# A causal convolution in front of two gated layers: two products of tile 1 made on GpSimd

## The chip, the core and the metric

The kernel runs on one core of a Trainium2 chip. A core has TensorE (matrix products, PE in the rows), VectorE (DVE), ScalarE (ACT), GpSimd (POOL), SyncE (SP, which issues the transfers here) and 16 DMA engines. All share one on-chip memory of 128 partitions (SBUF); TensorE writes its sums to a second one (PSUM, 8 banks). The metric is device microseconds of one execution of the whole kernel, median of several runs; lower is better.

## What is computed

```python
w = softmax(weight_gen, axis=-1)             # (2, 4096, 8 heads, 7 taps)
x_pad = concat([zeros((B, 6, D)), x], axis=1)
out[b, s, h, :] = sum_k w[b, s, h, k] * x_pad[b, s + k, h, :]   # 24 channels a head, D = 192
x = out.reshape(8192, 192)
x = (silu(x @ w_gate) * (x @ w_val)) @ w_out          # 192 -> 1536 -> 192
h = x @ w_in                                          # 192 -> 2048
return (h * clip(h + 3, 0, 6) / 6) @ w_out2           # 2048 -> 192
```

Each position gets its own seven tap weights for each of eight heads; the sum of the seven products goes through two layers. The layers' matrix products are made with each operand split into a high and a low part, so one product of the reference is three on TensorE.

## The kernel before

**Tiles and blocks.** The 8192 positions are 16 tiles of 512 (128 partitions x 4 positions, 768 numbers a partition). A tile's layer 1 is 12 blocks of 128 hidden columns, its layer 2 is 8 blocks of two such groups. The blocks run tiles 0 and 1 in turns of four (blocks 0 to 3 are tile 0's, 4 to 7 tile 1's), then tiles 2 and 3, then layer 2 of one tile and layer 1 of a later one in turn. In a layer 1 block TensorE makes `pg` and `pv` (L661, 18 matrix products, two at a time on the two halves of the array), ScalarE the silu (`p`, L695), VectorE multiplies by `pv` (L698), ScalarE makes the high part `gh` (L674), VectorE the low part `gl` (L703), and two or three blocks later TensorE multiplies these by `wo` (L742).

**Turns.** The two halves of the array write both banks in turn. `Turn` (L589) hands over: an empty instruction in GpSimd's queue waits for both halves' last product of the first part, and the second part on TensorE waits for that instruction. Each block has one or more, in block order, and apart from a few memsets at the start GpSimd has nothing else to do.

**Weights.** They come as float64 and are made into a high and a low fp32 part in chunks: ScalarE takes the exponent (L243), VectorE shifts (L249) and joins the words (L252, L258), ScalarE writes the high part (L309 for `wi`, L327 for `wo`), VectorE the low part (L294). A block waits for its chunk.

**Convolution.** A tap is one VectorE product of 128x768 (L390), 24 channels a weight. From tile 2 on the seven products are added on VectorE. Tiles 0 and 1 are needed before there is other work, and TensorE adds part of theirs: `TERMS[t]` lists groups of taps; within a group VectorE adds (L457), and each group's sum is a *term*, which TensorE multiplies by a unit matrix into two PSUM banks (L467, eight matrix products of fp32, 16 in the trace). Tile 1 has three terms, of taps 6+5, 4+3 and 2+1+0: seven products and four sums on VectorE.

**Order.** Everything is issued in an order that a planner in the kernel makes when it is built: it keeps a clock for each engine (`V["A"]`, `V["D"]`, `clock`), fills each engine's queue between a block's steps with items of the convolution (`c`) or of the weights (`w`), and puts terms into TensorE's queue when its clock has come to their time (`late_pe`). Each engine then works through its queue in order. While tile 1 has no term begun, the planner also fills time in which it expects TensorE to wait with products of the unit matrix that nobody reads (`heat`, L502, called at L624).

Of the kernel before, what the change touches and what calls it, by code (L numbers as in the profile page):

```python
# [8 lines left out]
F32 = mybir.dt.float32  # L9
# [29 lines left out]
def conv_swiglu_relu6_kernel(  # L39
# [11 lines left out]
    nc = tc.nc  # L51
    P = 128
    B, S, D = x.shape
# [12 lines left out]
    MJ = 4  # L66
# [2 lines left out]
    GBUFS = 4  # L69


    TERMS = [[[6], [5], [4], [3, 2], [1, 0]], [[6, 5], [4, 3], [2, 1, 0]]]

    START = [(0, 4), (4, 8), (8, 12)]
    SPREAD = (0, 4)
# [30 lines left out]
    V = {"A": 2000.0, "D": 2800.0, "Q": 1000.0}  # L106
    late_act, late_exp, late_pe, urgent = [], [], [], []
# [61 lines left out]
    def v_cost(cols):  # L169
        return 1.042 * cols + 70  # L170
# [40 lines left out]
    pools, late = {}, {}  # L211
# [166 lines left out]
    def after_taps(t):  # L378

        if t + 2 < T:  # L380
            before = load_x(t + 2)
            if before:
                before()
        if t == groups[t // GT][-1]:
            load_wg(t // GT + 2)

    def taps(eng, t, k, o, a=0, b=None):

        b = b or sizes[t]
        eng.tensor_mul(  # L390
            o.rearrange("p j (h g) -> p j h g", h=H),
            xt_t[t][:, a + k:b + k, :].rearrange("p j (h g) -> p j h g", h=H),
            wg_t[t][:, a:b, :, k:k + 1].broadcast_to([P, b - a, H, G]),
        )
# [39 lines left out]
    def conv_pe_items(t):  # L434


        n = sizes[t]
        box, count, items = {}, [0], []
        c = v_cost(n * D)

        def step(k, tag):
            def go():
                if tag == "acc":
                    o = vp.tile([P, MJ, D], F32, tag="acc", name="acc", bufs=1)
                else:
                    count[0] += 1
                    src = vp if count[0] % 2 else pools["c"]
                    o = src.tile([P, MJ, D], F32, tag="tmp", name="tmp", bufs=2)
                box[tag] = o
                taps(nc.vector, t, k, o[:, :n, :])  # L450
                if k == TERMS[t][-1][-1]:
                    after_taps(t)
            return go

        def add():
            o = box["tmp"][:, :n, :]
            nc.vector.tensor_add(o, o, box["acc"][:, :n, :])  # L457

        def pe(first, last):
            o = box["tmp"]  # L460

            def go():
                if first:
                    pe_t[t] = [acc_bank(0), acc_bank(2)[:D2]]
                for dst, a, b in zip(pe_t[t], (0, P), (P, D)):
                    for s in range(n):
                        nc.tensor.matmul(  # L467
                            dst[:, s * P:(s + 1) * P], o[:, s, a:b], ident,
                            start=first and s == 0, stop=last and s == n - 1,
                        )  # L470
            late_pe.append((go, V["D"]))

        for q, term in enumerate(TERMS[t]):
            items.append((c, step(term[0], "tmp")))
            for k in term[1:]:
                items += [(c, step(k, "acc")), (c, add)]
            _, f = items.pop()

            def both(f=f, first=q == 0, last=q == len(TERMS[t]) - 1):
                f()  # L480
                pe(first, last)
            items.append((c, both))
        return items
# [15 lines left out]
    def acc_bank(q):  # L499
        return ap.tile([P, MN], F32, tag=f"a{q}", name=f"a{q}")  # L500
# [389 lines left out]
    def due(q):  # L890
        tag = queues[q][0][0]
        if tag == ("c", 1):
            left = sum(x[0] == tag for x in queues["c"])
            return SPREAD[0] + SPREAD[1] * (1 - left / len(conv_pe_items(1)))
        return dues.get(tag, 0)
# [204 lines left out]
    with tc.manual_schedule():  # L1100
# [3 lines left out]
            c=w1.enter_context(tc.tile_pool(name="c1", bufs=2)),  # L1104
            n=768, ahead=4,
# [17 lines left out]
        add(("c", 0), s0)  # L1123
        until(("c", 0))
        taps0 = [(("c", 0), c, f, None) for c, f in conv_pe_items(0)]
        s1 = [(("c", -1), x[0], x[1], x[2] if len(x) > 2 else None) for x in s1]
        s2 = [(("c", -2), x[0], x[1], x[2] if len(x) > 2 else None) for x in s2]
        first = taps0[:1] + s1[:2] + taps0[1:]
# [18 lines left out]
        nc.scalar.activation(warm, three, AF.Silu)  # L1147
        on("A", 1300)
        add(("c", 1), conv_pe_items(1))
        queues["c"] += s2[2:]  # L1150
        add(("c", 2), conv_items(2))
# [4 lines left out]
        for ph in phases:  # L1156
            kind, t0, _ = ph[0]
            if kind == 2 and t0 + 4 < T:
                t = t0 + 4
# [46 lines left out]
```

## Time and profile before

| | |
|---|---|
| median of 3 runs (lowest to highest) | 1251.93 us (1250.68 to 1252.17) |
| profiled execution, its own time | 1249.53 us |
| span in its trace | 1247.5 us |
| TensorE busy | 1231.6 us, 99% |
| VectorE busy | 922.1 us, 74% |
| ScalarE busy | 674.9 us, 54% |
| GpSimd busy | 3.6 us |

A row of a timeline gives the start, the duration, the engine, the line, the operation and the tile names; in brackets stands the idle time before it and what ended that. Busy spans of neighbours may overlap by some hundredths, since an instruction starts before the one ahead has left. In the trace one fp32 matrix product by the unit matrix counts twice.

### The profile page before, as it was taken

The numbers are of one execution on the slowest core, as the hardware profiler recorded it, in microseconds if no ns is written. First come the engines' busy times: TensorE is split into PE (matmuls) and PEld (weight loads), VectorE is DVE, ScalarE is ACT, GpSimd is POOL, SyncE is SP. The second block draws the span as 40 slices with busy tenths as digits, with TensorE's granted clock in tenths as the row PEclk, the third lists the DMA queues.
The fourth block names the chain that finished last, engine by engine and source line by source line (L and its number), as shares of the span: only waits on it lengthen the run. The fifth ranks groups of instructions, "written<-read, shape, count | busy, mean of one in ns | idle before, by whom it ended". The sixth has DMA issues, their size and how long they took to land.

```text
span 1247.5 us, 29356 instructions
## 1 busy us (share of the span) xinstructions
PE 1231.6 (99%) x12104; PEld 1183.7 (95%) x12104; DVE 922.1 (74%) x1475; ACT 674.9 (54%) x1175; POOL 3.6 (0%) x11
## 2 busy tenths in 40 slices
PE   8899999999999999999999999999999999999998
PEld 7687878999999999999999999999999999999998
DVE  8889987986876848687595866959478694645665
ACT  3455565654655547465464546546465554645555
POOL 1000000000000000000000000000000000000000
PEclk9999999999999999999999999999999999999999
DMA  8313230011010100101001010100000000000000
GB/s 236 117 45 106 86 107 9 14 42 53 18 46 18 54 10 10 45 18 53 10 10 45 19 53 19 38 17 19 37 19 14 12 8 16 17 14 9 14 15 14
DMA packets 26725, 46.96 MB, mean 38 GB/s; under 512 B 3046, under 2 KB 19428, under 8 KB 26592
## 3 DMA queue, kind: packets, MB, share of 16 engines
q1 hardware_dynamic: 26592, 45.09, 12.3%
q8 instruction: 95, 1.56, 0.5%
q14 instruction: 38, 0.31, 0.1%
HBM read 30.92 MB, written 6.29 MB: 30 GB/s over the span
## 4 chain that ended last, share of the span: by engine, by line
PE 91%; DVE 5%; ACT 2%; DMA 1%; SPq 1%; issue 1%; DVEq 0%; ACTq 0%; POOLq 0%
PE ph L661 23%; PE a L822 21%; PE a L742 16%; PE pv L661 15%; PE pg L661 14%; DVE p L698 1%; DVE gl L703 1%; DVE f L252 0%; DMA xt<-in_x_dram 0%; DVE f L258 0%; DVE tmp L390 0%; ACT gh L674 0%; DMA raw<-in_moe_w_in_dram 0%; SPq L305 0%; DVE wi L294 0%
## 5 line engine op out<-in xcount | busy, mean ns | idle before, releaser
L661 PE MATMUL pg<-s,wi 64*128 64x512 f32 x1728 | 454.1, 395 | 6.1 <-ACT wi L309 2.5
L661 PE MATMUL pv<-s,wi 64*128 64x512 f32 x1728 | 425.1, 395 | 2.2 <-DVE p L698 1.1
L674 ACT ACTIVATE gh<-p 128x512 fp32r<-128x512 f32 x448 | 278.9, 633 | 216.9 <-DVE p L698 164.6
L661 PEld LDWEIGHTS pg<-s,wi 64*128 64x128 f32 x1728 | 307.1, 184 | 21.1 <-ACT wi L309 2.8
L661 PE MATMUL ph<-s,wi 64*128 64x512 f32 x2304 | 318.7, 393 | 1.2 <-DVE p L785 1.1
L661 PEld LDWEIGHTS pv<-s,wi 64*128 64x128 f32 x1728 | 297.1, 184 | 14.9 <-DVE p L698 2.5
L822 PE MATMUL a<-wo,gh 64*128 64x384 f32 x2016 | 311.0, 353 | 0.0
L822 PE MATMUL a<-wo,gl 64*128 64x192 f32 x2016 | 300.6, 247 | 0.0
L822 PEld LDWEIGHTS a<-wo,gh 64*128 64x128 f32 x2016 | 295.9, 184 | 0.3
L822 PEld LDWEIGHTS a<-wo,gl 64*128 64x128 f32 x2016 | 290.8, 187 | 0.0
L661 PEld LDWEIGHTS ph<-s,wi 64*128 64x128 f32 x2304 | 268.7, 184 | 3.3 <-DVE p L785 1.6
L742 PE MATMUL a<-gh,wo 64*128 64x512 f32 x1152 | 253.3, 392 | 0.8 <-ACT wo L327 0.7
L781 ACT ACTIVATE p<-ph,three 128x512 f32<-128x512 f32 x256 | 161.7, 684 | 126.5 <-PE ph L661 125.9
L698 DVE TENSOR_TENSOR p<-p,pv 128x512 f32<-128x512 f32 x192 | 131.8, 687 | 122.7 <-ACT p L695 121.5
L742 PE MATMUL a<-gl,wo 64*128 64x512 f32 x768 | 208.0, 392 | 0.0
L703 DVE TENSOR_TENSOR gl<-p,gh 128x512 fp32r<-128x512 f32 x192 | 132.6, 691 | 94.3 <-ACT gh L674 94.3
L695 ACT ACTIVATE p<-pg 128x512 f32<-128x512 f32 x192 | 114.5, 596 | 160.8 <-PE pg L661 159.7
L785 DVE SCALAR_TENSOR_TENSOR p<-p,ph 128x512 f32<-128x512 f32 x256 | 163.6, 680 | 46.2 <-ACT p L781 45.8
L795 DVE TENSOR_TENSOR gl<-p,gh 128x512 fp32r<-128x512 f32 x256 | 165.7, 689 | 13.1
L742 PEld LDWEIGHTS a<-gh,wo 64*128 64x128 f32 x1152 | 161.8, 184 | 9.0 <-ACT wo L327 1.4
L742 PEld LDWEIGHTS a<-gl,wo 64*128 64x128 f32 x768 | 115.7, 184 | 4.1
L390 DVE TENSOR_TENSOR tmp<-xt,wg 128x768 f32<-128x768 f32 x92 | 87.0, 953 | 0.7
(66 smaller groups left out, 509.1 us busy)
## 6 DMA issues: line engine op xcount, KB each, us to landing
xt<-in_x_dram SPq DMA_DIRECT2D x14, 960.0 KB, 4.9
out_dram<-o SPq DMA_DIRECT2D x15, 384.0 KB, 2.3
s<-s SPq DMA_DIRECT2D x16, 256.0 KB, 2.9
s<-s SPq DMA_DIRECT2D x56, 64.0 KB, 2.0
raw<-in_moe_w_out_dram SPq DMA_DIRECT2D x8, 384.0 KB, 3.2
raw<-in_moe_w_out_dram SPq DMA_DIRECT2D x3, 768.0 KB, 7.0
raw<-in_moe_w_in_dram SPq DMA_DIRECT2D x16, 128.0 KB, 2.4
wg<-in_weight_gen_dram SPq DMA_DIRECT2D x7, 224.0 KB, 5.0
```

The costliest lines, as they stand in the source:

```text
L390: eng.tensor_mul(o.rearrange("p j (h g) -> p j h g", h=H), xt_t[t][:, a + k:b + k, :].rearrange("p j (h g) -> p j h g", h=H), wg_t[t][:, a ...
L661: return nc.tensor.matmul(ps[b][:, :N], w[rows, s, m, c], x[rows, l, :N], start=start, stop=stop)
L674: nc.scalar.activation(gh[:, :N], p[:, :N], AF.Copy)
L695: nc.scalar.activation(p[:, :N], pg[:, :N], AF.Silu)
L698: nc.vector.tensor_mul(p[:, :N], p[:, :N], pv[:, :N])
L703: nc.vector.tensor_sub(gl[:, :N], p[:, :N], gh[:, :N].bitcast(F32))
L742: return nc.tensor.matmul(y[:, :N], wo1[rows, i, col:col + P], x[rows, :N], start=start, stop=stop)
L781: nc.scalar.activation(q, ph[:, :N], AF.Relu, bias=three)
L785: nc.vector.scalar_tensor_tensor(out=q, in0=q, scalar=6.0, in1=ph[:, :N], op0=ALU.min, op1=ALU.mult)
L795: nc.vector.tensor_sub(gl[:, :N], q, gh[:, :N].bitcast(F32))
L822: return nc.tensor.matmul(z[s][:, :w], x[rows, s * P:(s + 1) * P], late["wo2"][rows, blk, :w], start=start, stop=stop,)
```

## The change

Taps 1 and 0 leave tile 1's last term. GpSimd makes their two products into two tiles of their own (`pt`), and each becomes a term of its own for TensorE, put into its queue behind tile 1's first term. VectorE loses two products and two sums of 128x768; TensorE gets five terms of tile 1 in place of three. All other code is the same; since the planner's clocks move, the order around it does too.

```diff
-    TERMS = [[[6], [5], [4], [3, 2], [1, 0]], [[6, 5], [4, 3], [2, 1, 0]]]
+    TERMS = [[[6], [5], [4], [3, 2], [1, 0]], [[6, 5], [4, 3], [2]]]
+    POOL_TAPS = [[], [1, 0]]
...
+        pooled = []
+
+        def pool_taps():
+            for k in POOL_TAPS[t]:
+                o = pools["c"].tile([P, MJ, D], F32, tag="pt", name="pt", bufs=2)
+                taps(nc.gpsimd, t, k, o[:, :n, :])
+                pooled.append((o, V["D"] + 2400 * (len(pooled) + 1)))
...
-            late_pe.append((go, V["D"]))
+            late_pe.append((go, at or V["D"]))
+            if first:
+                for x, when in pooled:
+                    pe(False, False, x, when)
+
+        if POOL_TAPS[t]:
+            items.append((0, pool_taps))
```

On GpSimd the two products stand behind the turn of block 0 and ahead of the turn of block 1. They wait for the softmax weights of tile 1 (VectorE, L371).

On VectorE, from tile 1's first tap to the product `p` of block 1 (`wi_84<-f_239` is the low part of block 1's weights, `f_251` the chunk of blocks 2 and 3), before:

```order
L390 TENSOR_TENSOR tmp<-xt_131,wg_103 128x768
L390 TENSOR_TENSOR acc<-xt_131,wg_103 128x768
L249 TENSOR_SCALAR f_251<-f_251 128x768
L698 TENSOR_TENSOR p<-p,pv 128x512
L457 TENSOR_TENSOR tmp<-tmp,acc 128x768
L703 TENSOR_TENSOR gl<-p,gh 128x512
L294 SCALAR_TENSOR_TENSOR wi_84<-f_239,wi_84 128x3x128
L390 TENSOR_TENSOR tmp<-xt_131,wg_103 128x768
L390 TENSOR_TENSOR acc<-xt_131,wg_103 128x768
L457 TENSOR_TENSOR tmp<-tmp,acc 128x768
L698 TENSOR_TENSOR p<-p,pv 128x512
```

and now:

```order
L391 TENSOR_TENSOR tmp<-xt_131,wg_103 128x768
L391 TENSOR_TENSOR acc<-xt_131,wg_103 128x768
L250 TENSOR_SCALAR f_251<-f_251 128x768
L712 TENSOR_TENSOR p<-p,pv 128x512
L295 SCALAR_TENSOR_TENSOR wi_84<-f_239,wi_84 128x3x128
L717 TENSOR_TENSOR gl<-p,gh 128x512
L466 TENSOR_TENSOR tmp<-tmp,acc 128x768
L391 TENSOR_TENSOR tmp<-xt_131,wg_103 128x768
L712 TENSOR_TENSOR p<-p,pv 128x512
```

The low part of block 1's weights has moved ahead of a sum and of `gl`; one tap and one sum have left this stretch.

On TensorE, between blocks 1 and 2 (the last product of block 1, then the first two of block 2; `a_344` and `a_345` are the two banks of tile 1's sum), before:

```order
L661 MATMUL pg<-s_254,wi_84 128x512
L467 MATMUL a_344<-ident,tmp 128x128 x4
L467 MATMUL a_345<-ident,tmp 64x128 x4
L661 MATMUL pg<-s_254,wi_84 128x512
L661 MATMUL pv<-s_254,wi_84 128x512
```

and now:

```order
L675 MATMUL pg<-s_254,wi_84 128x512
L521 MATMUL a_383<-ident 128x128 x19
L675 MATMUL pg<-s_254,wi_84 128x512
L675 MATMUL pv<-s_254,wi_84 128x512
L675 MATMUL pg<-s_254,wi_84 128x512
```

Tile 1's first term has left this place, and 19 products that nobody reads stand there. The `heat` between blocks 0 and 1 has 8 of them in place of 13.

On TensorE, between blocks 2 and 3 (`pv<-s_254` is the last of block 2), before:

```order
L661 MATMUL pv<-s_254,wi_84 128x512
L467 MATMUL a_344<-ident,tmp 128x128 x4
L467 MATMUL a_345<-ident,tmp 64x128 x4
L661 MATMUL pg<-s_254,wi_84 128x512
L661 MATMUL pv<-s_254,wi_84 128x512
```

and now:

```order
L675 MATMUL pv<-s_254,wi_84 128x512
L476 MATMUL a_428<-ident,tmp 128x128 x4
L476 MATMUL a_429<-ident,tmp 64x128 x4
L476 MATMUL a_428<-ident,pt 128x128 x4
L476 MATMUL a_429<-ident,pt 64x128 x4
L476 MATMUL a_428<-ident,pt 128x128 x4
L476 MATMUL a_429<-ident,pt 64x128 x4
L675 MATMUL pg<-s_254,wi_84 128x512
```

Three terms stand where one stood. Behind block 3, where the third term stood, the two others stand now. From tile 1's first block on TensorE's order is the same as before.

## Rows read from the trace of the kernel before

**Rows 1.** The profile page: busy time, share of the span and instructions.

```profile
PE 1231.6 (99%) x12104; PEld 1183.7 (95%) x12104; DVE 922.1 (74%) x1475; ACT 674.9 (54%) x1175; POOL 3.6 (0%) x11
```

**Rows 2.** Stretches: length, busy time and instructions by engine, granted clock, DMA share, GB/s.

```profile
32.40:34.90 2.50, 0.00 (x0) 0.00 (x0) 2.06 (x5) 1.54 (x2) 0.00 (x0) 0.93 0.00 0
34.90:38.60 3.70, 3.07 (x12) 1.67 (x12) 3.24 (x4) 1.76 (x2) 0.00 (x0) 0.59 0.71 210
53.00:60.00 7.00, 7.00 (x64) 5.62 (x62) 6.86 (x10) 3.37 (x5) 0.00 (x0) 1.00 0.42 115
300.00:600.00 300.00, 300.00 (x3010) 299.16 (x3008) 218.54 (x346) 162.76 (x283) 0.00 (x0) 1.00 0.10 28
```

**Rows 3.** TensorE's timeline, blocks 1 to 4: start, duration, operation, idle before.

```profile
23.43 3.17 PE L507 MATMUL a<-ident 128*128 128x128 f32 x26
28.01 0.50 PE L661 MATMUL pg<-s,wi 64*128 64x512 f32 x1 [0.74 <-DVE wi L294]
29.32 0.18 PEld L661 LDWEIGHTS pv<-s,wi 64*128 64x128 f32 x1 [0.55 <-POOLq L598]
30.21 2.18 PE L467 MATMUL a<-ident,tmp 128*128 128x128 f32 x16
34.91 0.79 PE L661 MATMUL pg<-s,wi 64*128 64x512 f32 x1 [2.52 <-ACT wi L309]
38.64 1.56 PE L742 MATMUL a<-gh,wo 64*128 64x512 f32 x3 [0.67 <-ACT wo L327]
41.07 2.18 PE L467 MATMUL a<-ident,tmp 128*128 128x128 f32 x16
43.17 0.49 PE L661 MATMUL pg<-s,wi 64*128 64x512 f32 x1
47.64 2.18 PE L467 MATMUL a<-ident,tmp 128*128 128x128 f32 x16 [0.71 <-DVE tmp L457]
49.75 0.49 PE L661 MATMUL pg<-s,wi 64*128 64x512 f32 x1
```

**Rows 4.** VectorE's timeline from tile 1's first tap to block 1's `p`.

```profile
23.12 0.96 DVE L390 TENSOR_TENSOR tmp<-xt,wg 128x768 f32<-128x768 f32 x1
25.33 0.68 DVE L698 TENSOR_TENSOR p<-p,pv 128x512 f32<-128x512 f32 x1
25.93 0.95 DVE L457 TENSOR_TENSOR tmp<-tmp,acc 128x768 f32<-128x768 f32 x1
26.80 0.68 DVE L703 TENSOR_TENSOR gl<-p,gh 128x512 fp32r<-128x512 f32 x1
27.40 0.55 DVE L294 SCALAR_TENSOR_TENSOR wi<-f,wi 128x384 fp32r<-128x384 f32 x1
30.95 0.69 DVE L698 TENSOR_TENSOR p<-p,pv 128x512 f32<-128x512 f32 x1 [0.27 <-ACT p L695]
```

**Rows 5.** GpSimd's operations by line and shape: busy us, mean ns.

```profile
L151 POOL MEMSET xt<- 1x1152 f32 x2 | 2.1, 1050 | 0.1
masks.py:199 POOL TENSOR_SCALAR_AFFINE_SELECT ident<-ident 128x128 f32<-128x128 f32 x1 | 0.3, 292 | 0.1
```

**Rows 6.** Timeline of the start: GpSimd's memsets, a VectorE operation beside them, one without.

```profile
1.28 3.06 POOL L151 MEMSET xt<- 1x1152 f32 x4
...
3.24 0.39 DVE L359 TENSOR_TENSOR wg<-wg,sm 128x224 f32<-128x224 f32 x1
...
6.82 0.39 DVE L359 TENSOR_TENSOR wg<-wg,sm 128x224 f32<-128x224 f32 x1
```

**Rows 7.** TensorE's waits from 110 to 320 us: total, times, longest.

```profile
PE pv L661 <- DVE p L698: 0.9, 1, 0.9
PE pg L661 <- ACT p L695: 0.7, 1, 0.7
PE pv L661 <- DVE s L574: 0.4, 1, 0.4
...
PE ph L661 <- DVE p L785: 1.1, 1, 1.1
```

More of the change, by code (lines that the diff above doesn't have):

```diff
@@ L457, in add, with pe @@
             nc.vector.tensor_add(o, o, box["acc"][:, :n, :])
-        def pe(first, last):
-            o = box["tmp"]
+        def pe(first, last, o=None, at=None):
+            o = o or box["tmp"]
             def go():
```

## The prediction

> **What bounds the kernel.** I read the busy line first: TensorE is busy 99% of the span, VectorE 74%, and GpSimd has 3.6 us of work [rows 1]. That is an average, so the stretches come next. From 53 us on TensorE has hardly a gap, and in the long middle none at all [rows 2]; what it waits for behind 110 us is 0.9 + 0.7 + 0.4 + 1.1 us in the four largest waits [rows 7]. So the end of the kernel is the time at which TensorE comes to tile 1's first block, plus work that the change leaves alone. Every microsecond by which block 4, at 49.75 [rows 3], comes later or earlier is one at the end. Before that block TensorE does wait, and its timeline names whom for [rows 3]: 0.74 us for the low part of block 1's weights, 2.52 us for the weights of block 2, 0.67 us for `wo`, 0.71 us for a sum of tile 1's taps. All four come from VectorE's queue, directly or through ScalarE.
>
> **What VectorE gives back.** Up to `p` of block 0 at 25.33 its queue stays as it is. Then the low part of block 1's weights came at 27.40, behind a sum and `gl` [rows 4]; now it is next, at 25.93 where the sum started. That is 27.40 - 25.93 = 1.47 us earlier. The shorter `heat` does not eat it: 26 products took 3.17 us, 0.122 each [rows 3], so 16 end at 23.43 + 1.95 = 25.4. Block 1 then ends at 30.21 - 1.47 = 28.74 instead of 30.21, its `p` and the chain of words behind it (which the change leaves in the same order) come 1.47 us earlier too, and so do block 2's start, from 34.91 to 33.44, and the wait for `wo` at 38.64. The 19 new `heat` products take 38 x 0.122 = 4.64 us from 28.74 and end at 33.38, just inside the wait. Block 2 ends at 41.07 - 1.47 = 39.60. The other tap and sum that leave VectorE stood late, ahead of the third term: the 0.71 us at 47.64 goes, since the second and third terms' sums are then ready before block 3 ends. Together -2.18 us.
>
> The clock: in the 2.5 us without a product the granted clock fell, and the stretch after it ran at a mean of 0.59 of 2.4 GHz, part of it at the lower level [rows 2]. `heat` now fills that gap. I cost this at nothing: block 2's first part, the one that ran slowly, ended in a wait for `wo` (0.67 us before 38.64), which VectorE's chain ends.
>
> **What TensorE gets.** A term takes 43.17 - 41.07 = 2.10 us [rows 3]. Before, the first of tile 1's three stood at 30.21 to 32.39, ahead of the wait that ended at 34.91: it cost nothing, the wait was its cover. That place now holds `heat`. All five terms now stand where TensorE has work behind them: three between blocks 2 and 3 where one stood, two behind block 3 where one stood. That is three more on the path, 3 x 2.10 = +6.30 us. Sum so far: 6.30 - 2.18 = +4.12 us at block 4.
>
> **What comes later.** VectorE has four operations of 0.95 us less, and TensorE is later. Behind 110 us the waits for `p` and its ScalarE part are 0.9 + 0.7 us [rows 7], at a place where convolution and weights crowd VectorE. They stand at a transposition that takes two of the four banks, so part remains whatever VectorE does. Bounds 0 and -1.6; I take -0.5, since the same crowd of weight steps stands there now, nearer to the first. The planner's new order could also add such a wait.
>
> **What the two products cost GpSimd.** No row shows a two-input product there. Below, VectorE's own tap: 0.96 us [rows 4]. The nearest GpSimd rows: a memset of 1152 numbers 1.05 us, which reads nothing, and a select of 128 in 0.292 us, which reads one input [rows 5]. Scaled by columns the select gives 768 / 128 x 0.292 = 1.75 us; twice that for two inputs, 3.5 us, is the upper bound. I take 1.75 us, the row on this engine that reads and writes. Both products together: 3.5 us from 23.1, until 26.6. What is queued behind them on GpSimd is block 1's turn: TensorE's second part of block 1 waits for it. It was taken at 29.32 after 0.55 us [rows 3], so it is asked for at 28.77 - 1.47 = 27.3. At 1.75 us each the products are through by then; at 3.5 us each they end at 30.1, and block 1 would be 2.8 us later.
>
> **What they cost VectorE.** Both engines then read SBUF at once, and no row shows that. The memsets ran beside a VectorE operation that took 0.39 us, as it did without them [rows 6], but a memset reads nothing. Bounds: no cost; or one engine at a time, both products whole ahead of block 1's weights, 2 x 1.75 = +3.5 us. I take sharing, each at half pace while both read: VectorE's work from 23.12 to the end of that low part is 26.48 - 23.12 = 3.36 us, of which 0.60 is `p`, which reads PSUM; the other 2.76 us doubles. The low part is 2.76 us later, GpSimd is done at about the same time (29.5 us), and block 1's turn is not later than its weights. I take this value rather than none because the work beside which the row shows no cost is of another kind, and rather than 3.5 because `p` leaves one gap. Everything behind, block 2 and its `wo`, hangs on that chain and takes the +2.76 us whole.
>
> Sum: 4.12 - 0.5 + 2.76 = **+6.4 us**. On the profiled execution's 1249.53 us that is 1255.9. The runs' median lies 2.4 us above that execution, so the forecast against it is 1251.93 + 6.4 = 1258.3 us.
>
> **A rule against the change.** In the trace before, VectorE and GpSimd never read SBUF together, and the memset beside `L359` cost nothing [rows 6]. The Trainium skill, "SBUF — State Buffer", section "Who interferes with whom", says that a VectorE instruction with two SBUF inputs contends with a GpSimd instruction that reads SBUF, though not with one that only writes it, and that the one which starts first holds the interface while the other fully blocks. The memset row agrees with its second half; no run here shows the first. By it the sum would be that of the first rival.
>
> **Rivals.** *One at a time.* An engine that has started holds the memory to the end of its instruction. The tap at 23.12 starts first, GpSimd's first product comes in behind it and its second behind VectorE's next: +3.5 us on the chain instead of 2.76, +7.1 us in all, 1259.0. If VectorE's back-to-back queue wins until `p` at 25.33, the second product waits until VectorE idles (about 30.1), block 1's turn with it until 31.9, and block 1 ends 0.55 + 0.89 us later at 33.3 instead of 28.74: +4.6, in all +8.2 us, 1260.1. For it: most of VectorE's queue there has two inputs in SBUF. Against it: nothing in the rows.
>
> *No interference.* +4.12 - 0.5 = +3.6 us, 1255.5. It needs products of under about 2.1 us each, or the turn is late.
>
> *Not slower: relief behind 110 us.* With no interference as well, VectorE's queue is so much shorter that all four late waits go, 0.9 + 0.7 + 0.4 + 1.1 = 3.1 us instead of 0.5 [rows 7]: 4.12 - 3.1 = +1.0 us, 1252.9. It decides if no wait for `p` is left at those places. Against it: the banks at the transpositions are taken as before.
>
> *Slow products.* 3.5 us each on GpSimd, and sharing: VectorE reads for 2.76 us up to the low part and for 2.34 more in `gl`, sum and tap, 5.1 in all, which take 10.2; with `p` that is until 33.9, when GpSimd has done 5.7 of 7.0 us. Its turn comes at 35.2, and block 1 ends 0.55 + 0.89 us later at 36.6 instead of 28.74: +7.9 us in place of 2.76, in all +11.5 us, 1263.4.
>
> **How the numbers follow.** Sharing 0.32, one at a time 0.25, no interference 0.20, relief 0.15, slow products 0.08. Sharing and one at a time lie within 2 us of each other, so the forecast is 1258.3. The range goes from 1253.5, between relief and no interference, to 1261.5, above one at a time: relief and slow products are left out, some 0.2. About 0.2% (2.5 us) is what a measurement of this kernel can tell from no change. Slower by more: sharing, one at a time, slow products and 0.12 of no interference, 0.77. Within it: 0.08 of no interference, whose 3.6 us may lose another 1.1 to a second late wait, and 0.09 of relief, 0.17. Faster by more than that: the rest of relief, if VectorE's queue also held TensorE back where no wait shows, 0.06.
>
> **What the profile after will show.** The two `pt` products on GpSimd near 23 us, with their duration. VectorE's rows beside them at 0.95 or longer. The wait for block 2's weights ending at 33.4 without interference, at 36 or more with it. Three terms in a row between blocks 2 and 3 and two behind block 3, 2.1 us each, without a wait of 0.71. Tile 1's first block at 49.75 + 4.1 to + 8.7. The rest at the same pace. I am wrong if TensorE finds idle time under the added terms, or if block 4 starts by 51 us.

## The result, and the profile after

The changed kernel takes 1259.68 us (median of 4 runs, 1259.03 to 1260.60) where the kernel before took 1251.31 us (4 runs, 1250.66 to 1252.17): a ratio of 1.0070 with a 95% interval of 1.0056 to 1.0084, slower by 8.4 us where 6.4 was forecast. The profiled execution's own time is 1259.27 us, its span 1257.5 us.

The busy line of the changed kernel's page answers to [rows 1].

```profile
PE 1242.3 (99%) x12164; PEld 1192.9 (95%) x12164; DVE 921.7 (73%) x1471; ACT 676.7 (54%) x1175; POOL 8.1 (1%) x13
```

VectorE has four instructions less and yet only 0.4 us less busy time; GpSimd has 4.5 us more. What the products did beside VectorE stands in the timelines of the two engines, first GpSimd's and then VectorE's, which answers to [rows 4].

```profile
23.87 4.47 POOL L391 TENSOR_TENSOR pt<-xt,wg 128x768 f32<-128x768 f32 x2 [19.51 <-DVE wg L372]
```

```profile
23.76 0.96 DVE L391 TENSOR_TENSOR tmp<-xt,wg 128x768 f32<-128x768 f32 x1
24.64 2.30 DVE L391 TENSOR_TENSOR acc<-xt,wg 128x768 f32<-128x768 f32 x1
26.86 1.90 DVE L250 TENSOR_SCALAR f<-f 128x768 int32<-128x768 int32 x1
28.68 0.67 DVE L712 TENSOR_TENSOR p<-p,pv 128x512 f32<-128x512 f32 x1
29.28 0.54 DVE L295 SCALAR_TENSOR_TENSOR wi<-f,wi 128x384 fp32r<-128x384 f32 x1
```

In the kernel before, the second tap and the shift were these rows:

```profile
24.00 0.95 DVE L390 TENSOR_TENSOR acc<-xt,wg 128x768 f32<-128x768 f32 x1
24.86 0.55 DVE L249 TENSOR_SCALAR f<-f 128x768 int32<-128x768 int32 x1
```

The second tap took 2.30 us in place of 0.95, the shift 1.90 in place of 0.55: 1.35 us more each. The first tap, `p` and the low part of the weights kept their times. From the first tap's start to the low part's start it is now 5.52 us. Without the products it would be 25.93 - 23.12 = 2.81 us, by [rows 4] and the new order. So the products cost VectorE 2.71 us at this place.

TensorE's timeline of the same kernel, answering to [rows 3]:

```profile
32.06 4.51 PE L521 MATMUL a<-ident 128*128 128x128 f32 x38
36.76 0.50 PE L675 MATMUL pg<-s,wi 64*128 64x512 f32 x1 [0.19 <-ACT wi L310]
...
40.49 1.55 PE L756 MATMUL a<-gh,wo 64*128 64x512 f32 x3 [1.55 <-ACT wo L328]
...
42.91 3.77 PE L476 MATMUL a<-ident,tmp 128*128 128x128 f32 x16
46.61 4.28 PE L476 MATMUL a<-ident,pt 128*128 128x128 f32 x32
...
54.51 4.28 PE L476 MATMUL a<-ident,tmp 128*128 128x128 f32 x32
58.72 0.50 PE L675 MATMUL pg<-s,wi 64*128 64x512 f32 x1
```

The 19 idle products (matrix products by the unit matrix that nobody reads) end at 36.57, the weights of block 2 come 0.19 us later; the wait for `wo` is 1.55 us in place of 0.67; three terms stand in a row behind block 2 and two behind block 3, the latter without idle time ahead. One of the five took 3.77 us, not 2.18. The granted clock says why, in this row of stretches (columns as in [rows 2]):

```profile
42.90:46.60 3.70, 3.70 (x17) 3.15 (x16) 3.18 (x5) 1.92 (x3) 0.00 (x0) 0.54 0.26 92
```

0.54 of 2.4 GHz: nearly all of that stretch ran at 1.2 GHz, some microseconds behind the idle 1.55 us. (The 8 idle products ahead of block 1 ran at 1.2 GHz too in this execution, 3.78 us in place of the 2.05 of experiment 2; the wait for block 1's weights hid it.) Set against [rows 3], the timeline gives an account of the span, place by place:

| place | before | after | later by | what was added on the way |
|---|---|---|---|---|
| tile 1's first tap on VectorE | 23.12 | 23.76 | 0.64 | the start: VectorE waits 0.5 us for a transfer of `x` in this execution, not in that of before |
| block 2 | 34.91 | 36.76 | 1.85 | -1.47 (order) + 2.71 (products) |
| `wo` in block 2 | 38.64 | 40.49 | 1.85 | nothing |
| block 3 | 43.17 | 50.82 | 7.65 | two terms, 4.2, and 1.6 for the term at 1.2 GHz |
| the terms behind block 3 | 47.64 | 54.51 | 6.87 | the gap of 0.71 us is gone |
| block 4 | 49.75 | 58.72 | 8.97 | one term, 2.1 |
| end of the span | 1247.5 | 1257.5 | 10.0 | 1.0 behind block 4 |

In their own times the two profiled executions differ by 9.7 us; that of before is one of its quicker ones, 1.8 us under the median of 1251.31, and that of after 0.4 us under its own, which leaves the 8.4 of the medians. Half of the last 1.0 us can be read from TensorE's waits from 62 to 300 us (total, times, longest), first of the kernel before, then of the changed kernel,

```profile
PE pg L661 <- ACT p L695: 1.3, 2, 0.7
PE pv L661 <- DVE p L698: 1.1, 2, 0.9
```

```profile
PE pv L675 <- DVE p L712: 2.0, 3, 1.2
PE pg L675 <- ACT p L709: 1.6, 2, 0.8
PE ph L675 <- DVE p L799: 1.1, 1, 1.1
```

4.7 us in the three largest groups; the kernel before has 1.3 + 1.1 + 1.1 = 3.5 us in the same groups of that stretch (the third is in [rows 7]). Other waits are shorter in the changed kernel, so that TensorE's whole idle time behind block 4's start is 9.3 us in place of 8.8. The other half is busy time, 1189.45 us in place of 1188.98: the granted clock is 0.64 from 124 to 128 us, behind the longest of these waits, where the kernel before has 1.00.

### The profile page after: what moved, and what is told of

Same layout as the page of the kernel before. It is cut to its first block, busy times and chain, and to the rows that moved or that the text cites. A ratio compares the mean times of both kernels' runs of the same rounds, so it can differ in the third digit from the quotient of the medians.

```text
span 1257.5 us, 29482 instructions
## 1 busy us (share of the span) xinstructions
PE 1242.3 (99%) x12164; PEld 1192.9 (95%) x12164; DVE 921.7 (73%) x1471; ACT 676.7 (54%) x1175; POOL 8.1 (1%) x13
## 4 chain that ended last, share of the span: by engine, by line
PE 88%; DVE 5%; ACT 1%; issue 1%; DMA 1%; SPq 0%; DVEq 0%; ACTq 0%
PE ph L675 22%; PE a L836 21%; PE pv L675 15%; PE a L756 15%; PE pg L675 12%; DVE p L712 1%; DVE f L253 1%; DVE gl L717 1%; ACT gh L688 1%; DVE f L259 0%; DVE acc L416 0%; DMA raw<-in_moe_w_out_dram 0%; DVE f L250 0%; DVE tmp L391 0%; DMA raw<-in_moe_w_in_dram 0%
## 5 line engine op out<-in xcount | busy, mean ns | idle before, releaser
L836 PE MATMUL a<-wo,gh 64*128 64x384 f32 x2016 | 307.9, 353 | 0.0
L836 PE MATMUL a<-wo,gl 64*128 64x192 f32 x2016 | 297.6, 248 | 0.0
L836 PEld LDWEIGHTS a<-wo,gh 64*128 64x128 f32 x2016 | 289.2, 184 | 0.4
L836 PEld LDWEIGHTS a<-wo,gl 64*128 64x128 f32 x2016 | 287.1, 187 | 0.0
L675 PEld LDWEIGHTS ph<-s,wi 64*128 64x128 f32 x2304 | 265.9, 184 | 3.3 <-DVE p L799 1.6
```

The lines of the kernel that those rows point to most:

```text
L675: return nc.tensor.matmul(ps[b][:, :N], w[rows, s, m, c], x[rows, l, :N], start=start, stop=stop)
L836: return nc.tensor.matmul(z[s][:, :w], x[rows, s * P:(s + 1) * P], late["wo2"][rows, blk, :w], start=start, stop=stop,)
```

## Experiments

Each kernel ran beside the kernel before on one chip, and its ratio is against those runs of before, whose median lay between 1251.4 and 1252.1 us. The expectations are quoted as they stood before the runs; "after" below is the changed kernel, 1259.7 us. A difference from after is one of medians from different occasions; by the ratios it comes out 0.2 to 1.7 us larger, so it is known to a microsecond or so. Experiments 1, 2 and 6 ask what the products do to VectorE, 3, 5, 7, 8 and 9 what a term costs at its place, 4, 10, 11 and 12 what the clock costs.

### 1. The products alone, in the kernel before

```diff
+    GHOST = [[], [1, 0]]
...
+        def ghost():
+            for k in GHOST[t]:
+                o = pools["c"].tile([P, MJ, D], F32, tag="pt", name="pt", bufs=2)
+                taps(nc.gpsimd, t, k, o[:, :n, :])
```

> The kernel before, with the two GpSimd products made at the same place, which nothing reads: VectorE's, TensorE's and ScalarE's orders are those of before, and the output is the reference's. Theory (GpSimd and VectorE take turns, one instruction at a time, each product about 1.35 us once it has its turn): two VectorE instructions between 24 and 28 us are 1.35 us longer each, the others are not, and TensorE's wait ahead of block 1 grows by about 2.7 us: 1254.0. Rival 1 (both run at once, each at half its pace, as the prediction had it): about 2.7 us too, but spread over every VectorE instruction that lies beside a product, four or five of them by 0.4 to 0.8 us each. Rival 2 (the products cost VectorE nothing, and the longer rows of after come from its other order): 1251.3.

Measured: 1256.33 us, ratio 1.0037 (1.0023 to 1.0051), by the ratio 4.6 us over before. VectorE's timeline has after's pattern to the hundredth, in before's order:

```profile
24.04 2.30 DVE L392 TENSOR_TENSOR acc<-xt,wg 128x768 f32<-128x768 f32 x1
26.27 1.90 DVE L251 TENSOR_SCALAR f<-f 128x768 int32<-128x768 int32 x1
```

Two instructions are longer by 1.35 us each, and the tap ahead of them, beside which GpSimd's first product already stands in the trace, keeps its 0.96 us: turns, not sharing, and the size is that of the theory. TensorE's timeline shows why the whole kernel lost more than 2.7 us:

```profile
30.75 0.79 PE L670 MATMUL pg<-s,wi 64*128 64x512 f32 x1 [3.44 <-DVE wi L296]
...
34.52 3.26 PE L469 MATMUL a<-ident,tmp 128*128 128x128 f32 x16
39.22 0.49 PE L670 MATMUL pg<-s,wi 64*128 64x512 f32 x1 [1.45 <-ACT wi L311]
```

The wait for block 1's weights grew from 0.74 to 3.44 us, by 2.70. Behind it the rest of block 1 took 34.52 - 30.75 = 3.77 us where [rows 3] have 30.21 - 28.01 = 2.20, and block 2 starts 4.3 us later (39.22 against 34.91), 2.70 + 1.57. A second such stretch lies over the term at 46.44, which took 3.97 us. In this execution the wait that VectorE made was paid twice: once as the wait, and once in the clock behind it (0.51 from 30 to 34 us).

### 2. A fill in place of each product

```diff
-                taps(nc.gpsimd, t, k, o[:, :n, :])
+                nc.gpsimd.tensor_mul(
+                    o[:, 0, :G], xt_t[t][:, k, :G], wg_t[t][:, 0, 0, k:k + 1].broadcast_to([P, G])
+                )
+                nc.gpsimd.memset(o[:, :n, :], 0.0)
```

> The changed kernel, but in the place of each product GpSimd multiplies 24 columns and fills the whole tile with zeros by a memset; every other engine's order is that of the changed kernel. Left out: taps 1 and 0 of tile 1 are missing from its sum. Theory (it is the two-operand reading of a product that shuts VectorE out): the tap, sum and shift between 24 and 28 us are back at 0.96, 0.95 and 0.55 us, the first term starts 2.7 us earlier: 1257.0. Rival (any GpSimd instruction of that size on SBUF shuts VectorE out, a fill too): the sum and the shift stay 0.9 us or more longer, 1258 to 1259.7.

Measured: 1257.15 us, ratio 1.0045 (1.0029 to 1.0061): 2.5 us under after, where 2.7 was expected. GpSimd's and VectorE's timelines:

```profile
23.22 0.94 POOL L461 TENSOR_TENSOR pt<-xt,wg 128x24 f32<-128x24 f32 x1 [18.88 <-DVE wg L372]
24.22 0.74 POOL L464 MEMSET pt<- 128x768 f32 x1
24.91 0.61 POOL L461 TENSOR_TENSOR pt<-xt,wg 128x24 f32<-128x24 f32 x1
```

```profile
23.99 0.98 DVE L391 TENSOR_TENSOR acc<-xt,wg 128x768 f32<-128x768 f32 x1
24.90 0.55 DVE L250 TENSOR_SCALAR f<-f 128x768 int32<-128x768 int32 x1
...
25.96 0.55 DVE L295 SCALAR_TENSOR_TENSOR wi<-f,wi 128x384 fp32r<-128x384 f32 x1
```

The fill at 24.22 lies wholly beside the tap and lengthens it by 0.03 us at most. The products of 24 columns show the other side: 0.94 and 0.61 us beside VectorE, where the same size takes 0.22 us when VectorE is idle (experiment 6). So the product, which reads SBUF, takes turns with VectorE, and the fill, which only writes, does not; an instruction of GpSimd that reads one operand was not tried. The low part of the weights comes at 25.96, where the prediction put it without interference (25.93). In the profiled execution only 1.5 of the 2.7 us are left at block 4, since the clock fell sooner behind the wait for `wo` (0.50 from 38 to 42.9 us).

### 3. The products made, their terms left out

```diff
-                    pe(False, False, x, when)
+                    late_pe.append((lambda: None, when))
```

> The changed kernel with the products made and TensorE's two terms that sum them left out; all else stands in the same order. Left out: taps 1 and 0 of tile 1 are missing from its sum. Theory (a term lies on the path with its full 2.10 us, whatever comes behind): 1259.7 - 2 x 2.1 = 1255.5 if the one term that is left there still runs at half clock (3.8 us). Rival (part of it is given back, since VectorE or ScalarE is late for what follows, as the prediction had it with 0.5 us of later waits): 1256 to 1257.5.

Measured: 1256.77 us, ratio 1.0045 (1.0031 to 1.0058): 2.9 us under after, not 4.2. The rival is right. Rows of TensorE and of ScalarE:

```profile
42.88 2.18 PE L476 MATMUL a<-ident,tmp 128*128 128x128 f32 x16
...
48.67 4.28 PE L476 MATMUL a<-ident,tmp 128*128 128x128 f32 x32
56.48 0.50 PE L675 MATMUL pg<-s,wi 64*128 64x512 f32 x1 [3.53 <-ACT s L538]
```

```profile
54.52 0.63 ACT L688 ACTIVATE gh<-p 128x512 fp32r<-128x512 f32 x1 [2.00 <-DVE p L712]
```

TensorE is through with tile 1's sums at 52.95 and then waits 3.53 us for ScalarE to round them. ScalarE has the rounding behind `gh` of block 3, and that behind `p`, which VectorE reaches at 53.81, behind the softmax of tiles 2 and 3 and the weights. So in after's order the two terms are on the path with 2.9 of their 4.2 us, by the medians; the rest is cover for VectorE. The theory's condition did not hold in this execution, where the term that is left took 2.18 us and not 3.8: TensorE came to the last terms 5.3 us earlier than in after's profile, and to block 4 only 1.7 us earlier (each less its late start).

### 4. Idle products in the wait for `wo`

```diff
         begin(b)
+        if b == 2:
+            issue(list(pushed))
+            heat(6, 2)
```

> The changed kernel with six more idle matmuls of TensorE between block 2's first part and its wait for the weights of its second part (1.55 us in the changed kernel); only these are added, in the wait. Theory (the first term between blocks 2 and 3 takes 3.8 instead of 2.2 us because TensorE stood idle ahead of it and its clock was lowered): the term is back at about 2.2 us, 1259.7 - 1.6 = 1258.1. Rival 1 (the clock falls for another reason, as the stretch ahead at half clock): the term stays at 3.8 us, 1259.7. Rival 2 (the term gets shorter, but what follows waits for VectorE or ScalarE instead): 1259 to 1259.7 with a new wait in block 3.

Measured: 1258.10 us, ratio 1.0051 (1.0038 to 1.0065), 1.6 us under after, though the two intervals overlap. The term is back at its time:

```profile
39.93 1.60 PE L521 MATMUL a<-ident 128*128 128x128 f32 x12
41.51 1.55 PE L756 MATMUL a<-gh,wo 64*128 64x512 f32 x3
...
43.92 2.18 PE L476 MATMUL a<-ident,tmp 128*128 128x128 f32 x16
```

In this execution block 1 and the idle products behind it ran at 1.2 GHz instead (30 to 34 us: 0.50), behind the wait of 3.1 us for block 1's weights. That the idle time ahead of the term lowered its clock is likely, not shown: in five of the profiled executions (after and experiments 2, 5, 6 and 9) an idle 1.54 or 1.55 us ahead of `wo` was followed by a stretch at 1.2 GHz, and with the wait filled, here and in experiment 12, it was not; but in experiment 11 no such stretch followed the same 1.55 us. How much of the kernel's time the filling returns is not settled either.

### 5. After's order without the products

```diff
-    SPREAD = (0, 4)
+    SPREAD = (1, 3)
```

> No GpSimd product: the kernel before with tile 1's taps placed as late among VectorE's other work as in the changed kernel (the shift of block 1's weights ahead of the first sum), and so with the changed kernel's idle matmuls ahead of block 2 and its three VectorE terms at the same places: one between blocks 2 and 3, two behind block 3. All seven taps stay on VectorE. It shows what the changed kernel's order is worth without its products. Theory (each term has its price of 2.1 us when nothing hides it, block 1 is 1.47 us earlier, the gap of 0.71 us ahead of the last term goes): -1.47 + 2.1 - 0.71, which is -0.1: 1251.4, or up to 1.3 us less if filling the wait for block 2's weights with idle matmuls also keeps the clock at 2.4 GHz in block 2: 1250. Rival (VectorE, with two more taps and two more sums to do there than in the changed kernel, is late for the last term): 1253 to 1255.

Measured: 1254.67 us, ratio 1.0016 (1.0003 to 1.0030), 2 to 3 us slower than before. The rival is right (1.64 us is its wait):

```profile
40.73 3.82 PE L467 MATMUL a<-ident,tmp 128*128 128x128 f32 x16
...
52.00 2.18 PE L467 MATMUL a<-ident,tmp 128*128 128x128 f32 x16 [1.64 <-DVE tmp L457]
```

The first term ran at 1.2 GHz as in after, and VectorE is 1.64 us late for the last. So part of after's loss is not GpSimd's at all: the new order, which takes the first term out of the wait for block 2's weights, costs this much without any product. The figure holds the term's 2.1 us, its slow clock and VectorE's longer wait against the 1.47 us won at block 1; the run does not price them singly. And VectorE does need help there, which is what the products were to give.

### 6. The products later

The two products wait for VectorE to finish the output weights, by a small product of GpSimd that reads them; their terms stand behind block 3.

```diff
+                if not pooled:
+                    w = wo1[:, 0, D + D2:D + D2 + 24].bitcast(F32)
+                    nc.gpsimd.tensor_mul(o[:, 0, :24], w, w)
                 taps(nc.gpsimd, t, k, o[:, :n, :])
...
+                if last:
+                    for x, _ in pooled:
+                        sums(x)
...
+        if b == 2:
+            pool_late[1]()
```

> The changed kernel with GpSimd's two products held back until VectorE has finished the output weights of blocks 0 to 3 (a product of 24 columns that reads them stands ahead of the two), and with their two terms behind block 3 beside the others. All else stands in the changed kernel's order. Theory (products and VectorE take turns; a product has 1.35 us of its own): the tap, the sum and the shift at 24 to 28 us are back at about 0.95, 0.95 and 0.55 us, the first product meets VectorE idle (1.9 us in the changed kernel) and takes about 1.4 us there, the second lengthens one VectorE instruction by 0.8 to 1.35 us: 1259.7 - 2.7 + 0 to 1.0, so 1257 to 1258. Rival (VectorE's delay at 24 us was hidden by the wait for block 2's weights and the loss is the terms alone): 1259 to 1260.

Measured: 1257.67 us, ratio 1.0046 (1.0032 to 1.0060), 2.0 us under after and inside the theory's range. GpSimd's timeline, its product by tile, and VectorE's timeline:

```profile
39.67 0.22 POOL L464 TENSOR_TENSOR pt<-wo 128x24 f32<-128x24 f32 x1 [35.32 <-PE a L769]
39.97 3.04 POOL L391 TENSOR_TENSOR pt<-xt,wg 128x768 f32<-128x768 f32 x2
```

```profile
L391 POOL TENSOR_TENSOR pt<-xt,wg x2: 1542/1543/1544, 40.0 to 41.5; 128x768 f32<-128x768 f32 x2
```

```profile
40.94 0.69 DVE L725 TENSOR_TENSOR p<-p,pv 128x512 f32<-128x512 f32 x1 [2.80 <-ACT p L722]
41.55 2.28 DVE L391 TENSOR_TENSOR acc<-xt,wg 128x768 f32<-128x768 f32 x1
```

A product that does not wait takes 1.54 us. The first (from 39.97) found VectorE idle, and then beside `p`, whose second operand comes from PSUM: neither was lengthened. The second started at 41.47, VectorE's tap at 41.55: the tap took 2.28 us, its own 0.95 behind 1.33 of waiting. In after's trace a product is listed with 2.25 us: its own time and its wait for the tap ahead of it. A listed span of either engine contains its turn of waiting.

### 7. The three terms in the wait for block 2's weights

```diff
+        if b == 2:
+            run_pe()
         begin(b)
```

> The changed kernel with its first term and the two terms of GpSimd's products moved into the wait for block 2's weights, in the place of the 19 idle matmuls that stand there; products and VectorE's order are the changed kernel's. Theory (a term costs what no wait covers): three terms are 6.3 us in a wait of 4.7 us, so 1.6 us of them stay on the path in place of 6.3 and of the 1.6 us of the lowered clock, less what block 3's rounding then waits for VectorE: between 1259.7 - 6 and 1259.7 - 3, so 1253.7 to 1256.7; VectorE's delay of 2.7 us stays. Rival (TensorE's place does not matter, VectorE's total work up to tile 1's rounding sets the end): 1258 or more.

Measured: 1249.94 us, ratio 0.9985 (0.9975 to 0.9996): 9.7 us under after, and a little under before. It gained 4 us more than the best case of the theory.

```profile
29.20 0.49 PE L675 MATMUL pg<-s,wi 64*128 64x512 f32 x1 [3.09 <-DVE wi L295]
...
34.91 4.28 PE L476 MATMUL a<-ident,pt 128*128 128x128 f32 x32
...
41.05 1.56 PE L756 MATMUL a<-gh,wo 64*128 64x512 f32 x3 [0.27 <-ACT wo L328]
...
46.74 4.28 PE L476 MATMUL a<-ident,tmp 128*128 128x128 f32 x32
50.95 0.50 PE L675 MATMUL pg<-s,wi 64*128 64x512 f32 x1
```

Block 2 starts at 39.13, 3.0 us later than after's 36.76 - 0.64; but the wait for `wo` shrinks from 1.55 to 0.27 us, because `wo` does not come later, and the 3.77 + 4.28 us between blocks 2 and 3 are gone: -8.05 - 1.28 + 3.0 = -6.3 us, most of the 7.1 us by which block 4 starts earlier (50.95, where after, less its late start, has 58.08). Another 1.2 us lie behind block 4 (the rest of the span is 1197.55 us against 1198.78), where the three groups of waits are back at 1.1 + 1.1 + 1.1 us: the planner's clocks have moved again, and from 55 to 600 us VectorE's order is, instruction by instruction, that of the kernel before and not after's. The theory had counted the term's surplus, not the second wait that the surplus hides.

### 8. Better places, all taps on VectorE

Terms of two, one and four taps, the first two in the waits of block 2, the last behind block 3.

```diff
-    TERMS = [[[6], [5], [4], [3, 2], [1, 0]], [[6, 5], [4, 3], [2, 1, 0]]]
+    TERMS = [[[6], [5], [4], [3, 2], [1, 0]], [[6, 5], [4], [3, 2, 1, 0]]]
-    SPREAD = (0, 4)
+    SPREAD = (1, 3)
...
+        if b == 2:
+            heat(9, 2)
+            late_pe.pop(0)[0]()
         begin(b)
+        if b == 2:
+            issue(list(pushed))
+            run_pe()
```

> No GpSimd product: the kernel before, with tile 1's taps as late as in the fifth experiment, in three terms of two, one and four taps; nine idle matmuls and the first term in the wait for block 2's weights, the second term in the wait for the output weights in block 2, the last behind block 3. Theory (the place of a term decides, and short idle times of TensorE cost clock behind them): one term of 2.1 us less on the path, block 1 earlier by 1.47 us, block 2 at 2.4 instead of 1.2 GHz (1.3 us), less up to 1.5 us that VectorE is late for a last term of four taps: -3 to -5, so 1246.5 to 1248.5, faster than both. Rival (VectorE is late for the four taps by all that was won): 1250 to 1252.

Measured: 1253.74 us, ratio 1.0014 (1.0002 to 1.0025). The theory is wrong, by more than the rival said:

```profile
49.91 3.98 PE L467 MATMUL a<-ident,tmp 128*128 128x128 f32 x16 [4.74 <-DVE tmp L457]
```

TensorE waits 4.74 us for VectorE's four taps, and the term behind took 3.98 us. With the terms covered, VectorE is the bound up to tile 1. Experiment 7 has the products, hides its terms too, and takes 3.8 us less: the two differ in more than this, so what GpSimd's help alone is worth there is not shown.

### 9. Covered terms, and products behind block 1's weights

As experiment 7, with the wait of experiment 6 on block 1's weights in place of `wo`.

```diff
+                if not pooled:
+                    w = wi1[:, 0, 1, P:P + 24].bitcast(F32)
+                    nc.gpsimd.tensor_mul(o[:, 0, :24], w, w)
                 taps(nc.gpsimd, t, k, o[:, :n, :])
...
+        if b == 1:
+            pool_late[1]()
```

> The seventh experiment (three terms in the wait for block 2's weights), with GpSimd's products held back until VectorE has written block 1's weights, by a product of 24 columns that reads them; every other engine's order is that of the seventh. Theory (a product makes VectorE wait for as long as it runs, 1.35 us at each of two instructions, and it matters what stands behind these): block 1's weights come at 26.0 instead of 28.6 us and TensorE's wait of 3.1 us ahead of them shrinks to 0.4 us; the products then lengthen two of the instructions at 26.7 to 30 us, so block 2's weights come 2.7 us later than without products, where the three terms cover it; the stretch at 1.2 GHz behind the wait of 3.1 us goes too. Block 2 starts at about 36 instead of 39.1 us: 1249.9 - 3.1 = 1246.8, faster than both kernels. Rival (the order behind block 3 is bound by VectorE's taps and rounding, which do not come earlier): 1249 to 1250.

Measured: 1249.32 us, ratio 0.9974 (0.9964 to 0.9984). It is a little faster than both kernels, by 3 us against before and 10 against after, but by the rival's size rather than the theory's.

```profile
26.64 0.50 PE L685 MATMUL pg<-s,wi 64*128 64x512 f32 x1 [0.40 <-DVE wi L295]
...
31.90 4.28 PE L475 MATMUL a<-ident,pt 128*128 128x128 f32 x32
...
39.55 1.60 PE L766 MATMUL a<-gh,wo 64*128 64x512 f32 x3 [1.55 <-ACT wo L328]
...
46.78 4.28 PE L487 MATMUL a<-ident,tmp 128*128 128x128 f32 x32
```

The first half of the theory holds: block 1's wait is 0.40 us, and the terms end at 36.18. The 3 us so won are lost again: the wait for `wo` is back at 1.55 us, and the stretches from 38 to 46 us ran at 0.87 and 0.71 of the clock, so that the last terms start at 46.78 as in experiment 7.

### 10 and 11. Idle products in the longest wait

In experiment 7's kernel ahead of block 1, and in the kernel before ahead of block 2:

```diff
+        if b == 1:
+            heat(12, 2)
```

> The seventh experiment, with 12 more idle matmuls ahead of block 1, in its wait of 3.1 us for block 1's weights. Theory (TensorE's clock is lowered behind such a wait, for block 1 there): block 1's second part and the first term run at 2.4 GHz throughout, 1.0 us less for the one and 0.2 for the other: 1248.7. Rival (the lowered clock has another cause or falls elsewhere): 1249.9, or more where the idle matmuls run past the weights' coming.

```diff
+        if b == 2:
+            heat(9)
```

> The kernel before, with nine idle matmuls in its wait of 2.52 us for block 2's weights, behind the term that stands there; nothing else differs. Theory (the 1.2 GHz of 34.9 to 38.6 us is the price of that wait): block 2's first part takes about 1.75 us instead of 3.06, and 1.3 us less remain at the end: 1250.1. Rival (what block 2 gains there is lost to the wait for the output weights, which come no earlier): 0.67 us of wait ahead of them become 1.9 us, and the time stays at 1251.4.

Measured: experiment 10 1249.01 us, ratio 0.9981 (0.9970 to 0.9993), near the 1248.7 of the theory but not to be told from experiment 7's ratio. In its profiled execution the clock is 1.00 from 22 to 110 us. Experiment 11: 1251.85 us, ratio 0.9991 (0.9980 to 1.0002), 0.1 us under before by the medians and 1.1 by the ratio, which does not tell the rival (no change) from the theory (1.3 us less). Its timeline shows the rival's mechanism:

```profile
34.91 0.49 PE L661 MATMUL pg<-s,wi 64*128 64x512 f32 x1 [0.32 <-ACT wi L309]
...
38.64 1.56 PE L742 MATMUL a<-gh,wo 64*128 64x512 f32 x3 [1.55 <-ACT wo L327]
...
41.06 2.17 PE L467 MATMUL a<-ident,tmp 128*128 128x128 f32 x16
```

Block 2's first part runs at 2.4 GHz and is done earlier; the wait for `wo` takes all of it, and every start from 38.64 to block 4's is that of [rows 3], to 0.01 us. So up to block 4 the slow stretch at that place cost the kernel before nothing, as the prediction said. The same rows show 1.55 us of idle time that no slow stretch followed (clock 1.00 from 22 to 62 us).

### 12. Experiment 9 with six idle products in the wait for `wo`

```diff
         begin(b)
+        if b == 2:
+            issue(list(pushed))
+            heat(6, 1)
```

> The ninth experiment (three terms in the wait for block 2's weights, products held back until block 1's weights are written), with six more idle matmuls in block 2, in the wait of 1.55 us for the output weights. Theory (behind that wait the ninth ran at 0.71 to 0.87 of the clock from 38 to 46 us, which made block 3 about 1.7 us longer, and VectorE's last term is ready at 46.1 us, 0.7 us ahead of its place): block 3 at 2.4 GHz, the last two terms 0.7 to 1.7 us earlier, 1249.3 - 0.7 to 1.7: 1247.6 to 1248.6, with fewer slow-clock executions. Rival (the clock falls elsewhere instead, or VectorE's taps hold the last term): 1249.3.

Measured: 1250.67 us, ratio 0.9991 (0.9980 to 1.0001), not the theory's time. Its profiled execution does what was expected (1247.74 us, clock 1.0, the last terms at 45.16, 1.6 us earlier than in experiment 9); most of its twelve executions do not. Their mean granted clocks go from 0.993 to 1.0, and the slowest, at 0.993, takes 1253.5 us. The idle time that one profile shows does not decide in which executions the clock falls, and what does was not found.

## Why the prediction was right, step by step

- **VectorE gives back 2.18 us: right.** Experiment 2 shows it without the interference: the low part at 25.96 (forecast 25.93), block 2 at 33.46 (33.44). The gap of 0.71 us ahead of the last term is gone, since two sums left VectorE; in experiment 5, where they stay, it is 1.64.
- **Three more terms on the path, 2.10 us each: right in the profile of after,** 4.2 us between blocks 2 and 3 and 2.1 behind block 3, without idle time under them. It is not a price that a term always has. Two terms less return 2.9 us (experiment 3), and three that are moved under a wait return more than their time (experiment 7). The step that the prediction made well is the one on cover: the first term had been free only by its place.
- **What they cost VectorE, 2.76 us by sharing: the size was right by luck, the mechanism wrong.** It was 2.71 us, in turns: two waits of 1.35 us, where the prediction doubled 2.76 us of VectorE's own reading. The rival "one at a time" had the course exactly, GpSimd's first product behind the first tap and its second behind the next; with 1.35 us for each wait instead of 1.75 its total comes to 7.1 - 0.8 = 6.3, the forecast again. The Trainium skill, "SBUF — State Buffer", section "Who interferes with whom", has this as the exclusive lock; experiments 1 and 6 show it (1.33 to 1.35 us). Experiment 2 agrees with the other half of that section of the Trainium skill, that a GpSimd instruction which only writes does not contend with a VectorE instruction with two inputs in SBUF (0.98 us beside the fill), and `p` in experiment 6 with its exemption of a VectorE instruction with at most one input in SBUF (0.69 us). The shift has one operand and was made to wait all the same; the Trainium skill's exemption there leaves out VectorE's two-port modes, and no row shows in which mode the shift ran.
- **A product on GpSimd, 1.75 us: 1.54** (experiment 6). The turn of block 1 was not late, as forecast: the products end at 23.87 + 4.47 = 28.34, ahead of the weights at 29.28.
- **Later waits, -0.5 us: wrong in sign.** The three groups have 4.7 us in place of 3.5. VectorE has less to do, but the planner's new order put work elsewhere. Experiment 7, with the same products and VectorE in before's order there, has 3.3, which puts it down to the order and not to the products. The prediction had said that the planner could add such a wait and priced it at nothing. Its rows [rows 7] are not all of the stretch from 110 to 320 us either: there the first two groups have 1.1 and 1.3 us, with a second wait each.
- **The clock, nothing: right for the place that was argued, wrong for the kernel.** Experiment 11 bears out that the slow stretch in front of `wo` cost nothing. But the change made TensorE's idle time ahead of `wo` 1.55 us, in front of three terms, where nothing hides a slow stretch: 1.6 us in the profiled execution, and 1.6 by the medians of experiment 4, whose interval overlaps after's. That the idle time brought the slow stretch is likely, not shown.

Block 4 came 8.97 us later, 8.3 less the late start of 0.64, inside the 4.1 to 8.7 that the prediction named. Between the two profiled executions the sum missed by 3.0 us: 10.0 less the late start of 0.64 is 9.4 in place of 6.4. The last two terms are that: 1.5 us for what lies behind block 4 (1.0 in place of -0.5) and 1.6 for the clock. Between the medians it missed by 2.0, since before's profiled execution was a quick one. Taken one at a time, the order (experiment 5, 2.0 to 3.2 us), VectorE's waits (experiment 2, 2.5) and the two products' terms (experiment 3, 2.9) come to 7.4 to 8.6 of the 8.4 us; they act on each other, so that this is a rough check and no proof.

## What to carry to other kernels

A piece of work that TensorE does for another engine is free only under a wait; when a change adds such pieces, find the wait first and put them there, for the same two products cost 8.4 us or saved 1.5 to 3 us, against the kernel before, by where they and their sums stand. Before work goes from VectorE to GpSimd, ask which VectorE instructions stand beside it and what hangs on them: here a two-input product made a tap or the shift wait for nearly its whole length (1.35 of 1.54 us), though not `p`, which reads PSUM, so put it where VectorE idles, or behind what others are waiting for. When TensorE idles longer, add to the wait what the clock may cost behind it, and compare means of many executions.

## What the runs showed of the hardware

- GpSimd's product of 128x768 fp32 took 1.54 us undisturbed, 1.6 times VectorE's 0.95; beside VectorE both are listed longer (2.25 and 2.30 us), since each span contains the wait for the other's instruction.
- A VectorE instruction with only one operand, the shift of 128x768 int32 (0.55 us alone), was made to wait like the taps (1.90 us).
- Executions of one kernel differ with the granted clock. The kernel before ran 32 times beside experiments 5 to 8, from 1248.8 to 1255.3 us, with mean clocks from 0.998 to 0.992; a line through them has 0.9 us for each thousandth. So one kernel's executions spread by 0.5%, as much as most of the edits here, and the longer ones have the lower clock.
- The same idle time of TensorE was not followed by the same clock: behind 1.54 or 1.55 us ahead of `wo` a stretch at 1.2 GHz came in five of six profiled executions (not in experiment 11).
